# Threshold attention and a SoLU feed-forward block: extra matmuls into unread PSUM tiles before round 0 and in rounds 0 to 10

## The chip, the cores and the metric

The kernel runs on one core of a Trainium2 chip. The metric is device time in microseconds (us) of one execution; lower is better. A few per mille are enough to count here: three executions of the kernel before lie between 901.93 and 902.74 us.

## The reference

Attention over 8 batches of 8 heads, 576 positions of width 64, in float32, keeps only scores that lie within `tau` of their row's maximum. The result, seen as 4608 tokens of width 512, goes through a feed-forward block with a SoLU activation and a layer norm:

```python
scores = scale * np.matmul(q, k.transpose(0, 1, 3, 2))
thresh = np.max(scores, axis=-1, keepdims=True) - tau
scores = np.where(scores >= thresh, scores, -1000000000.0)
scores = scores - np.max(scores, axis=-1, keepdims=True)
attn = np.exp(scores)
attn = attn / (np.sum(attn, axis=-1, keepdims=True) + 1e-09)
x = np.matmul(attn, v)                  # then (B,H,S,D) -> (B*S, H*D)
h = x @ w_in                            # 512 -> 1024
solu = h * softmax(h)
ln = (solu - mu) / np.sqrt(var + 1e-06) * g_ln
out = ln @ w_out                        # 1024 -> 512
```

The weights `w_in` and `w_out` arrive as 64-bit floats; the kernel turns their bits into float32 on the chip.

## The kernel before

**Rounds.** The order of all work is written out by hand: one Python loop (L757 to L880) issues a round at a time, and every engine executes its own part of it in the order in which it was issued. There are 144 rounds with scores (`NS`), 18 for each batch; a round handles 128 query rows of two heads. After the last one the loop goes on until the feed-forward work is finished. In round `rnd` the loop issues, in this order:

1. `scores(rnd)` (L379): TensorE multiplies into the two PSUM tiles `s0` and `s1`, first the last 64 key columns, then the 512 others. All matmuls of the kernel but one work on 64 by 64 quarters of the array, four of them side by side (two halves of the rows, two of the columns); each float32 matmul appears in the profile as two rows.
2. `maxes(rnd)` (L411, its instruction is L417): VectorE finds each row's threshold. `ramp` (L428) on ScalarE applies it; `exps` (L437) on ScalarE takes the exponential and its sum.
3. In rounds 0, 2 and 4 only: `whole_pair(1)`, `whole_pair(2)`, `whole_pair(3)` (L358). TensorE transposes q, k and the row ends of two heads (L273) into two PSUM tiles, and ScalarE copies the results out to SBUF, six copies in the order q, q, k, k, ends, ends (L306, L331, L347, L351), alternately from the first tile and the second. `whole_pair(0)` stands before the loop and shares its copies between ScalarE and VectorE.
4. `normalise(rnd - 1)` (L441) on GpSimd.
5. One quarter of a feed-forward tile, if one is under way: `ff_h` or `ff_o`. The first becomes ready for round 11, so in rounds 0 to 10 the variable `quarter` stays 0, `cur` and `prev` stay None and so does `step`.
6. `attend` (L474), if a unit's weights are due (`LAG_PV`), in rounds 5, 7, 9, 10, 12 and on: TensorE multiplies the transposed weights `wT` with v (L495), and ScalarE copies the result out (L517).
7. `blocks(rnd - 1)` (L451): VectorE transposes the weights in blocks (L459), and DMAs put them in place in odd rounds.
8. In rounds 0 to 15: the conversion of one 128x512 piece of the weights, `weight_b` and then the first part of the next, `weight_a` (L217 to L253), mostly on VectorE, with one step on ScalarE (L230).

**PSUM.** Besides `s0` and `s1` there are two more tiles of 128x1024, named `p0` and `p1`, each with one buffer. The list `pairs_free` says which are to be had:

```python
    def take(name):
        tag = pairs_free.pop(0)
        return tag, ps_mm.tile([P, 1024], F32, tag=tag, name=name)
```

Who takes a tile puts its name back at the end of the list when the last reader has been issued; whether that reader has also finished is left to semaphores, which the framework sets: the first writer of a tile waits until the earlier tile of that name has been read. `whole_pair` takes both and gives both back, `attend` takes one and `attended` gives it back, and `gains()` (L186, round 3) takes and returns one.

**Before the loop.** The loads of the first two heads are issued, then `constants()` makes the identity matrix `ident` on GpSimd, further loads follow, and then `whole_pair(0)`.

Of the kernel before, what the change touches and what calls it, by code (L numbers as in the profile page):

```python
# [8 lines left out]
F32 = mybir.dt.float32  # L9
# [7 lines left out]
P = 128  # L17
# [3 lines left out]
def kernel(  # L21
# [27 lines left out]
    nc = tc.nc  # L49
# [50 lines left out]
    def take(name):  # L100
        tag = pairs_free.pop(0)
        return tag, ps_mm.tile([P, 1024], F32, tag=tag, name=name)


    def fence(first):
        m = nc.gpsimd.memset(mark, 0.0)
# [60 lines left out]
    def constants():  # L167

        nc.gpsimd.memset(lim, 0.0)
        nc.scalar.activation(out=ntau, in_=lim, func=AF.Exp)  # L170
        make_identity(nc, ident)
        nc.gpsimd.memset(mhalf, -0.5)
        nc.gpsimd.memset(mone, -1.0)
        nc.gpsimd.memset(lim, -896.0 * 8388608.0)

        nc.vector.tensor_scalar(
            out=scl, in0=tau_t, scalar1=0.0, scalar2=SCALE, op0=ALU.is_ge, op1=ALU.mult
        )  # L180
        nc.vector.tensor_scalar(
            out=tau_t, in0=tau_t, scalar1=0.0, scalar2=104.0, op0=ALU.max, op1=ALU.min
        )
        nc.vector.tensor_scalar(out=ntau, in0=tau_t, scalar1=-1.0, scalar2=None, op0=ALU.mult)
# [248 lines left out]
    def exps(s):  # L433
        d = live[s]
        d["sm"] = sm = small.tile([P, 2], F32, tag="sm", name="sm")
        for x, w in enumerate(d["w"]):
            nc.scalar.activation(  # L437
                out=w, in_=w, func=AF.Exp, bias=ntau, scale=1.0, accum_out=sm[:, x : x + 1]
            )
# [244 lines left out]
    NS = len(slots)  # L684
    PER = NS // B
    LAG_PV = 3

    pv_due = []
    for s, (b, kind, hp, r) in enumerate(slots):
# [39 lines left out]
    with tc.manual_schedule():  # L729
        nc.scalar.dma_start(out=tau_t, in_=tau.partition_broadcast(P))  # L730
        load_qk(0, 0)
        weight_load(0)
        constants()
        for x in range(1, 3):
            weight_load(x)
        for nm in ("q", "k"):
            load_ends(0, nm, slice(2, H), nc.sync)
        load_qk(0, 1)
        nc.sync.dma_start(out=g_rows, in_=g_ln.rearrange("(c p) -> c p", p=P))
        whole_pair(0)  # L740


        pieces = {r: x for x, r in enumerate(range(16))}
        whole = {0: 1, 2: 2, 4: 3}
        for r, hf, parts in ((0, 0, (0,)), (1, 0, (1, 2)), (3, 1, (0,)), (5, 1, (1, 2))):
            load_at[r] = [lambda hf=hf, parts=parts: load_v(0, hf, parts)]

        ready = []
        rnd = 0
        prev = cur = None  # L750

        between, starts, turns = [], [], []
        quarter = 0
        w2_done = False

        begin, middle, late = {}, {}, {}
        while True:  # L757
            more = rnd < NS
            if not more and not (
                ready or cur or prev or between or pv_due or live  # L760
                or max([rnd - 1, *begin, *middle, *late]) >= rnd
            ):
                break
            for job in begin.pop(rnd, []):
                job()
            if rnd == NS:
                pairs_free += ["s0", "s1"]
                if prev is not None:
                    between.append(prev)
                    prev = None  # L770
                if quarter == 2:
                    between.append(cur)
                    cur = None
                    quarter = 0
                assert quarter != 3
            if (
                cur is None and quarter == 0 and ready and ready[0][0] <= rnd
                and (more or len(between) < 3)
            ):
                cur = ready[0][1].pop(0)  # L780
                if not ready[0][1]:
                    ready.pop(0)
            busy = cur is not None or prev is not None
            items = []
            if more:
                room = SPARE
                if busy and quarter > 1 and preps and rnd + 4 < first_slot(preps[0][3]):
                    room = 0
                while preps and preps[0][0] <= rnd and preps[0][1] <= room:
                    _, n, make, _ = preps.pop(0)  # L790
                    items.append(make())
                    room -= n
                scores(rnd, items)
                maxes(rnd)
                ramp(rnd, 0)
                if rnd == 0:
                    weight_a(0)
                keeps(rnd, 0)
                keeps(rnd, 1)
                ramp(rnd, 1)  # L800
                exps(rnd)
            if rnd in whole:
                whole_pair(whole[rnd])
            if rnd - 1 in live:
                normalise(rnd - 1)
            for job in middle.pop(rnd, []):
                job()
            due = bool(pv_due) and pv_due[0][0] <= rnd
            step = None
            if quarter < 2 and cur is not None:  # L810
                step = ("h", quarter)
            elif quarter == 3:
                step = ("o", 1)
            elif not more:
                if between and ffn[between[0]].get("turned", NS + rnd) <= rnd:
                    prev = between.pop(0)
                    step = ("o", 0)
            elif quarter == 2 or (prev is not None and not due):
                if prev is None or (ffn[prev].get("turned", NS + rnd) <= rnd and w2_done):
                    step = ("o", 0)  # L820

            attending = None
            if due and (step is None or step[0] == "h") and len(pairs_free) > (step == ("h", 0)):
                attending = pv_due.pop(0)[1]
            if step == ("h", 0):
                ff_h(cur, 0, rnd + 1 < NS)
                quarter = 1
            elif step == ("h", 1):
                ff_h(cur, 1, None)
                quarter = 2  # L830
                late.setdefault(rnd, []).append(lambda t=cur: (ff_max(t), ff_exp(t)))
                late.setdefault(rnd + 1, []).append(lambda t=cur: (ff_mul(t), ff_sum(t)))
                middle.setdefault(rnd + 2, []).append(lambda t=cur: ff_stats(t))
                late.setdefault(rnd + 2, []).append(lambda t=cur: ff_norm(t))
                middle.setdefault(rnd + 3, []).append(lambda t=cur: (ff_norm2(t), ff_swap(t)))

                at = rnd + 4 if more or not ready else rnd + 6
                late.setdefault(at, []).append(lambda t=cur, at=at: ff_turn(t, at))
                if not more:
                    between.append(cur)  # L840
                    cur = None
                    quarter = 0
            elif step == ("o", 0):
                if prev is not None:
                    ff_o(prev, 0)
                quarter = 3
            elif step == ("o", 1):
                if prev is not None:
                    ff_o(prev, 1)
                    begin.setdefault(rnd + 1, []).append(lambda t=prev: ff_out(t))  # L850
                    late.setdefault(rnd + 1, []).append(lambda t=prev: ff_store(t))
                prev, cur = cur, None
                quarter = 0
            if attending is not None:
                attend(attending)
                attended(attending)
                b, kind, hp = attending
                if kind == 2 and b % 2:
                    ready.append((rnd + 1, [(b // 2,)]))
                elif kind < 2 and hp == NP - 1:  # L860
                    ready.append((rnd + 1, [(b, kind, 0), (b, kind, 1)]))
            if rnd - 1 in live:
                blocks(rnd - 1)
            for job in late.pop(rnd, []):
                job()
            if rnd == 3:
                gains()
            if rnd in pieces:
                x = pieces[rnd]
                weight_b(x)  # L870
                if x + 3 < len(pieces):
                    weight_load(x + 3)
                if x + 1 < len(pieces):
                    weight_a(x + 1)
            for job in load_at.pop(rnd, []):
                job()
            if rnd - 1 in pieces:
                weight_d(pieces[rnd - 1])
                w2_done = pieces[rnd - 1] == NW - 1
            rnd += 1  # L880
# [33 lines left out]
```

## Time and profile before

| what | value |
|---|---|
| median of three executions | 902.25 us (901.93 to 902.74) |
| the profiled execution, its own time | 902.25 us |
| its span, first to last instruction | 900.4 us |
| mean granted TensorE clock | 0.975 of full |
| TensorE matmul busy | 847.8 us (94%) |
| VectorE busy | 680.1 us (76%) |
| ScalarE busy | 591.9 us (66%) |
| GpSimd busy | 452.7 us (50%) |

PE is the matmul row of TensorE, PEld its weight loads, DVE is VectorE, ACT ScalarE, POOL GpSimd, SP the engine that issues most DMAs. Times in the timeline are in us from the start of the span: a row gives start, duration, engine, line, operation, the tiles written and read, shapes and count, and in brackets the idle time before it with what ended it. A start of round n is told here by the first of the two L417 rows of that round: 10.51 us for round 0, 15.27 for round 1, 21.25, 26.79, 32.13, 37.42, 43.86 for rounds 2 to 6, 104.59 for round 16.

### The profile page before, as it was taken

The page shows a single profiled execution, that of the slowest core. Times are in us where ns is not written, and L with a number is a line of the kernel's source. Part 1 is how long each engine was busy: PE and PEld are TensorE (multiplying, and loading weights), DVE is VectorE, ACT ScalarE, POOL GpSimd, SP SyncE. Part 2 cuts the span into 40 slices and gives each one's busy share as a digit, 9 for nine tenths or more (in the row PEclk, how much of TensorE's full clock was granted, in tenths as well). Part 3 has the DMA queues.
Part 4 walks back from the last instruction along what each step waited for, and adds up shares of the span by engine and source line. Part 5 has one row for each costly group of instructions (what it writes and reads, how often), then busy time and mean ns, then how long its engine had stood idle before and what let it go on. Part 6 is the DMA issues. An engine that isn't in the chain of part 4 may idle for free. (4 is left out here: it accounts for less than half of the span.)

```text
span 900.4 us, 39661 instructions
## 1 busy us (share of the span) xinstructions
PE 847.8 (94%) x17089; PEld 658.4 (73%) x17089; DVE 680.1 (76%) x1307; ACT 591.9 (66%) x1239; POOL 452.7 (50%) x870
## 2 busy tenths in 40 slices
PE   5667889999899999999999999999999999999997
PEld 3444677778688777877678787888778888777555
DVE  5999878878677777777777877777877877787351
ACT  5776767767677766777666766777767766666121
POOL 2556555555455555555545555555545555555120
PEclk8678899999999999999999999999999999999999
DMA  7999878886867777876767777876877766766322
GB/s 240 238 244 264 208 188 204 190 192 165 195 163 173 164 173 173 183 179 163 187 146 178 179 159 183 184 176 155 192 173 174 178 135 149 169 142 136 79 48 48
DMA packets 95502, 154.61 MB, mean 172 GB/s; under 512 B 27224, under 2 KB 69216, under 8 KB 95328
## 3 DMA queue, kind: packets, MB, share of 16 engines
q1 hardware_dynamic: 94336, 150.22, 70.5%
q8 instruction: 134, 2.20, 1.1%
q10 hardware_dynamic: 992, 1.87, 0.6%
q14 instruction: 40, 0.33, 0.1%
HBM read 46.14 MB, written 9.44 MB: 62 GB/s over the span
## 5 line engine op out<-in xcount | busy, mean ns | idle before, releaser
L417 DVE CUSTOM_DVE_ANT_0 w<-s_ps,tau_t 128x576 f32<-128x576 f32 x288 | 206.6, 755 | 151.3 <-PE s_ps L400 122.9
L428 ACT ACTIVATE w<-s_ps,nth 128x576 f32<-128x576 f32 x288 | 207.7, 744 | 121.4 <-DVE nth L417 100.1
L651 PE MATMUL o_ps<-w,uT 64*64 64x256 f32 x4608 | 271.3, 376 | 1.9 <-issue 1.0
L651 PEld LDWEIGHTS o_ps<-w,uT 64*64 64x64 f32 x4608 | 227.9, 133 | 51.2 <-ACT xh L517 9.6
L549 PE MATMUL h_ps<-w,xh 64*64 64x512 f32 x1856 | 222.0, 592 | 4.4 <-issue 4.4
L447 POOL TENSOR_SCALAR w<-w,sm 128x576 f32<-128x576 f32 x288 | 217.8, 768 | 14.3
L437 ACT ACTIVATE w<-w,ntau 128x576 f32<-128x576 f32 x288 | 220.3, 772 | 0.0
L459 DVE STREAM_TRANSPOSE T<-w 128x576 f32<-128x576 f32 x288 | 205.7, 750 | 4.3 <-POOL w L447 4.0
L495 PEld LDWEIGHTS pv<-wT,v 64*64 64x64 f32 x5760 | 173.5, 136 | 32.9 <-issue 13.8
L400 PE MATMUL s_ps<-kT,qT 64*64 64x64 f32 (+1 forms) x2048 | 177.1, 422 | 16.3 <-ACT w L428 15.1
L549 PEld LDWEIGHTS h_ps<-w,xh 64*64 64x64 f32 x1856 | 127.0, 134 | 80.8 <-issue 34.0
L495 PE MATMUL pv<-wT,v 64*64 64x128 f32 (+1 forms) x5760 | 173.9, 264 | 7.2 <-DMA wT<-T 5.1
L444 POOL TENSOR_SCALAR sm<-sm 128x2 f32<-128x2 f32 x144 | 36.1, 251 | 270.1 <-ACT w L437 267.4
L445 POOL TENSOR_TENSOR sm<-sm,mone 128x2 f32<-128x2 f32 x144 | 107.7, 748 | 12.0
L400 PEld LDWEIGHTS s_ps<-kT,qT 64*64 64x64 f32 x2048 | 70.2, 139 | 23.7 <-ACT w L428 21.0
L613 ACT ACTIVATE V<-u,nb,rs 128x1024 f32<-128x1024 f32 x36 | 44.7, 1241 | 52.4 <-POOL nb L603 52.4
L517 ACT COPY xh<-pv 128x256 f32<-128x256 f32 x64 | 23.8, 371 | 70.1 <-PE pv L495 70.1
L437 ACT ACTIVATION_READ_ACCUMULATOR w<-w,ntau 128x1 f32 x288 | 57.0, 198 | 0.0
L639 DVE STREAM_TRANSPOSE uT<-V 128x1024 f32<-128x1024 f32 x36 | 44.0, 1221 | 10.8 <-DMA V<-u 10.7
L562 DVE TENSOR_REDUCE hm<-h_ps 128x1 f32<-128x1024 f32 x36 | 43.0, 1195 | 10.7 <-PE h_ps L539 5.7
L577 DVE TENSOR_TENSOR u<-h_ps,u 128x1024 f32<-128x1024 f32 x36 | 42.8, 1190 | 10.6 <-ACT u L571 10.6
L571 ACT ACTIVATE u<-h_ps,hm 128x1024 f32<-128x1024 f32 x36 | 40.3, 1119 | 13.1 <-DVE hm L562 6.9
(74 smaller groups left out, 626.7 us busy)
## 6 DMA issues: line engine op xcount, KB each, us to landing
wT<-T SPq DMA_DIRECT2D x288, 288.0 KB, 5.6
V<-u SPq DMA_DIRECT2D x144, 64.0 KB, 3.6
out_dram<-ob SPq DMA_DIRECT2D x72, 128.0 KB, 3.1
v<-in_v_dram SPq DMA_DIRECT2D x16, 512.0 KB, 6.4
v<-in_v_dram SPq DMA_DIRECT2D x32, 256.0 KB, 5.9
q<-in_q_dram SPq DMA_DIRECT2D x15, 512.0 KB, 6.2
k<-in_k_dram SPq DMA_DIRECT2D x15, 512.0 KB, 6.8
raw<-in_moe_w_out_dram SPq DMA_DIRECT2D x8, 512.0 KB, 6.8
```

Of the source, the lines that this page charges most:

```text
L400: nc.tensor.matmul(out=ps[h][ROWS[y], ks], lhsT=lhsT, rhs=d["kT"][ROWS[h], ks], start=True, stop=True,)
L417: nc.vector.tensor_tensor_reduce(out=w, in0=ps[:, 0:S], in1=tau_t.to_broadcast([P, S]), scale=1.0, scalar=BIG, op0=ALU.add, op1=ALU.min, a ...
L428: nc.scalar.activation(out=d["w"][x], in_=d["ps"][x][:, 0:S], func=AF.Prelu, bias=d["nth"][x], scale=-1.0, alpha=1.0e30,)
L437: nc.scalar.activation(out=w, in_=w, func=AF.Exp, bias=ntau, scale=1.0, accum_out=sm[:, x : x + 1])
L445: nc.gpsimd.tensor_tensor(out=sm, in0=sm, in1=mone, op=ALU.pow)
L447: nc.gpsimd.tensor_scalar(out=w, in0=w, scalar1=sm[:, x : x + 1], scalar2=1.0, op0=ALU.mult, op1=ALU.mult)
L459: nc.vector.transpose(out=T[:, :, r, h, :], in_=w)
L495: nc.tensor.matmul(out=to, lhsT=d["v"][ROWS[u], h0 + h, m ^ 4 * u if m < 8 else m], rhs=rhs, start=m == 0, stop=m == NK - 1,)
L549: mm = nc.tensor.matmul(out=h[ROWS[y], f], lhsT=x[ROWS[r], c, ROWS[y]], rhs=w1_parts[ROWS[r], c, part ^ r], start=part == 0 and c == 0, st ...
L613: nc.scalar.activation(out=V, in_=u, func=AF.Identity, bias=nb, scale=rs)
L639: nc.vector.transpose(out=uT, in_=d["V"].rearrange("p y (m x) -> p m y x", x=32))
L651: nc.tensor.matmul(out=d["o"][ROWS[z], 512 * r : 512 * r + 256], lhsT=d["uT"][ROWS[r], m].rearrange("p y x -> p (y x)"), rhs=w2[ROWS[r], m ...
```

## The change

A helper `stir` issues four matmuls, one for each quarter of the array, into a fresh tile of a given PSUM name. No instruction reads that tile. It is called six times before `whole_pair(0)`, on `s0`, with the identity matrix as both operands and 128 columns; and in rounds 0 to 10 on the tile that stands first in `pairs_free` (the name is not taken from the list), with the identity and 512 columns of the first pair's `kT`. The first call in a round stands between `exps` and `whole_pair`, whenever `quarter` is 0 or 3; it is called A here. The second stands between the choice of `step` and `attend`, when the round has neither a feed-forward step nor a unit to attend; it is called B.

```diff
+    def stir(tag, cols, rhs_of):
+        x = ps_mm.tile([P, 1024], F32, tag=tag, name="stir")
+        for r in range(2):
+            for y in range(2):
+                nc.tensor.matmul(
+                    out=x[ROWS[y], 512 * r : 512 * r + cols], lhsT=ident[ROWS[r], ROWS[y]],
+                    rhs=rhs_of(ROWS[r]), start=True, stop=True,
+                )
...
     LAG_PV = 3
+    STIRRED = 10
...
         load_qk(0, 0)
         weight_load(0)
         constants()
+        for _ in range(6):
+            stir("s0", P, lambda rows: ident[rows])
         for x in range(1, 3):
             weight_load(x)
...
                 keeps(rnd, 1)
                 ramp(rnd, 1)
                 exps(rnd)
+            if more and rnd <= STIRRED and not quarter % 3:
+                stir(pairs_free[0], SM, lambda rows: pairs[0]["kT"][rows, 0:SM])
             if rnd in whole:
                 whole_pair(whole[rnd])
...
                 prev, cur = cur, None
                 quarter = 0
+            if rnd <= STIRRED and step is None and attending is None:
+                stir(pairs_free[0], SM, lambda rows: pairs[0]["kT"][rows, 0:SM])
             if attending is not None:
                 attend(attending)
                 attended(attending)
```

`SM` is 512 and `P` is 128. A is issued in rounds 0 to 10, B in rounds 0 to 4, 6 and 8.

## The prediction

> **What bounds the kernel now.** I read first the 40 slices of the page, because the change touches only rounds 0 to 10, the first 70 us.
>
> ```profile
> PE   5667889999899999999999999999999999999997
> ...
> DVE  5999878878677777777777877777877877787351
> ...
> PEclk8678899999999999999999999999999999999999
> ```
>
> TensorE has idle stretches only in the first six slices (135 us), and there its granted clock is low too. VectorE is the full engine there. The table of busy time by stage sharpens this (busy us of PE, PEld, DVE, ACT, POOL, then the clock):
>
> ```profile
> 20.00:25.00 5.00, 4.55 (x94) 2.88 (x86) 4.89 (x11) 3.84 (x10) 2.99 (x4) 0.67 0.66 201
> ...
> 100.00:110.00 10.00, 10.00 (x264) 7.68 (x260) 6.92 (x11) 5.83 (x17) 3.11 (x6) 1.00 0.70 169
> ```
>
> From 20 to 100 us VectorE is busy 4.87 to 5.00 of every 5 us, but for 40 to 45 (4.13). From 100 to 160 us TensorE is busy 8.5 to 10.0 of every 10, and the page has it at 9 from there to the end. So the front is set by VectorE's own work, the rest by TensorE's. VectorE executes in order: idle time put before one of its instructions in the front moves everything after it, TensorE's full stretch included. Idle time that is already there is all that a faster TensorE can win back.
>
> Third, the timeline of the front, for what TensorE waits for.
>
> ```profile
> 15.27 0.76 DVE L417 CUSTOM_DVE_ANT_0 w<-s_ps,tau_t 128x576 f32<-128x576 f32 x1
> ...
> 16.39 0.35 ACT L347 ACTIVATE qe<-tp,scl 128x64 f32<-128x64 f32 x1
> ...
> 26.18 0.34 ACT L347 ACTIVATE qe<-tp,scl 128x64 f32<-128x64 f32 x1
> ...
> 26.57 0.22 PE L188 MATMUL g_ps<-ident,g_rows 8*128 8x8 f32 x1 [1.80 <-ACT qe L347]
> 26.79 0.75 DVE L417 CUSTOM_DVE_ANT_0 w<-s_ps,tau_t 128x576 f32<-128x576 f32 x1
> ...
> 37.39 0.34 ACT L347 ACTIVATE qe<-tp,scl 128x64 f32<-128x64 f32 x1
> ...
> 37.79 4.22 PE L495 MATMUL pv<-wT,v 64*64 64x128 f32 x72 [1.80 <-ACT qe L347]
> ...
> 41.68 2.24 PE L400 MATMUL s_ps<-kT,qT 64*64 64x64 f32 x16
> ...
> 43.86 0.76 DVE L417 CUSTOM_DVE_ANT_0 w<-s_ps,tau_t 128x576 f32<-128x576 f32 x1 [0.83 <-PE s_ps L400]
> ```
>
> The two PE rows that end in "ACT qe L347" are the first users of a `p` tile after a `whole_pair`: each waited until ScalarE had made the copy of the ends, the last one out of that tile. Today both stand behind the next round's scores, and nothing urgent is queued behind them.
>
> **The change, part by part.** *Price of a stir.* The same shape runs in `ff_h`: weight loads of four rows follow each other every 0.85 us at half clock (95.34, 96.19, 97.04) and every 0.43 at full clock (98.59, 99.02, 99.45). A stir has eight rows: 1.70 or 0.86 us. From an unhindered start of the scores to VectorE's max it is 2.18 at half clock (41.68 to 43.86; 2.23 in round 0) and 1.24 or so at full (the row at 109.78, 1.24 long, ended when the max of 111.06 began).
>
> *B in rounds 0, 2 and 4.* `whole_pair` has just given its tiles back, so B writes the first of them, and like the two rows above it must wait for the copy of the ends. Queued behind it on TensorE are the next round's scores; behind those VectorE's max, then ScalarE's ramp, and so on. Before, the scores ran during ScalarE's copies. The new start of the max is: end of the copy, 0.05 us of signal, stir, scores.
>
> - Round 0: 16.39 + 0.35 + 0.05 = 16.79. With 0.86 + 1.24 the max starts at 18.89, with 1.70 + 2.23 at 20.72, against 15.27: 3.6 to 5.4 later. Round 1 holds 0.55 us of VectorE idle time (its row at 17.27 waited for GpSimd) that takes up as much: 3.1 to 4.9.
> - Round 2: copy's end 26.52, from the max at 21.25 5.27, a chain of ScalarE's own work that moves with the max. New period 5.32 + 2.10 = 7.42, or 5.32 + 3.93 = 9.25, against 26.79 - 21.25 = 5.54: 1.9 to 3.7.
> - Round 4: copy's end 37.73, 5.60 after the max at 32.13. New period 7.75 to 9.58 against 5.29: 2.5 to 4.3.
>
> Which clock? TensorE idles before B from the end of `whole_pair` (A moves it later) to the copy: some 3.4 us in round 0, 2.5 in round 2, 4 in round 4. Rows of before: after 3.16 idle (18.14), 1.64 (28.43, after one tiny matmul) and 3.4 (56.07) the scores ran at half clock; even after 1.80 idle the 72 rows at 37.79 took 4.22 us against 2.23 for 72 at 100.74. After 1.59 (45.51) they ran at full. Hence I take mostly half: 3.6 for stir and scores together in rounds 0 and 4, 3.2 in round 2. That gives 16.79 + 3.6 - 15.27 - 0.55 = 4.6, 5.32 + 3.2 - 5.54 = 3.0 and 5.65 + 3.6 - 5.29 = 4.0: **11.6 us**; the ends are 7.5 and 12.9.
>
> [...]
>
> *Round 5.* A, then `attend`, then the scores of round 6, on the path today: VectorE idles 0.83 us at 43.86 because those 72 rows ran at half clock. At full clock 0.86 + 2.23 + 1.24 = 4.3 fits into VectorE's own 5.6 us and the 0.83 goes; at half clock 1.70 + 4.22 + 2.23 = 8.15 against 6.44 costs 1.7. TensorE has by then worked some 4 us on end, so I take a gain of 0.4.
>
> *All other stirs of the loop (11 A and 7 B less the three)*: nothing. In rounds 1, 3, 6 and 8 A and B stand where TensorE waits for ScalarE's ramp: 2.3 us after the max the last ramp ends, the scores end 1.2 to 2.2 later, under the 5.3 of the period. In rounds 7 and 9 `attend` and the next scores end 1.77 and 1.82 us before VectorE needs them, against 0.86 to 1.70 for A; in round 10 `attend` waits for a DMA (0.86 and 1.66 us) behind A. At half clock throughout that cover is thin: two stirs (3.4) plus scores (2.2) exceed 5.3 by 0.3 us, a round at most 0.4; I keep 1.0 in all for the upper end.
>
> *The six before the loop.* The identity is complete at 1.32, the first q lands at 4.8. A matmul of 64 columns at half clock lasts 0.31 us, so one of 128 about 0.42 and a stir, two waves of four, about 0.65, as the tile is the same each time: 6 x 0.65 = 3.9, from 1.4 to 5.3. At worst `whole_pair(0)` starts 0.6 late. Against that the transposes (1.1 us for 32) and the scores of round 0 may find the full clock: 2.23 - 1.24 = 1.0 gained. I take 0.5 gained, between -1.0 and +0.6.
>
> *Later.* In rounds 16 and 17 VectorE idles 2.67 and 1.44 us for TensorE, whose clock was half from 85 to 98 us. No stir is issued there; but windows may fall otherwise after a shift. I take 0.5 gained, between -2.0 and 0.
>
> *Sum:* 11.6 - 0.4 - 0.5 - 0.5 = **10.2 us**. The profiled execution took 902.25 (span 900.4 and 1.85 around), which is also the median: **912.5**. Low ends: 7.5 - 0.8 - 1.0 - 2.0 = 3.7, 906; high ends: 12.9 + 1.7 + 0.6 + 1.0 = 16.2, 918.5.
>
> **The rivals.** *Warm and unhindered (faster):* B doesn't wait for the copies in effect, say because only unread columns matter, and the warm clock pays. It is bounded by VectorE's idle time: 1.0 in round 0, 0.83 at 43.86, up to 2.67 and 1.44 later: 896.3 to 900.4, say 899. It decides if B can start before about 12 us in round 0. Against it: B writes all 512 columns of both halves, the copies read columns 0 to 575, and the wait is seen twice. 0.06.
>
> *No change:* the delay is taken up before the end, because the full stretch of TensorE isn't tied to the front. For it speaks only that TensorE still idles 2.7 us between 120 and 140; every round follows the one before on each engine. 902. 0.04.
>
> *Slower, at full clock:* the stirs do keep the clock up, and stir and scores take 2.1 each time: 7.5 - 0.8 - 1.0 = 5.7, 908. 0.2.
>
> *Slower, the cover gone as well:* half clock throughout, rounds 1, 3 and 6 go over and `attend` in round 5 costs: 916 to 920. 0.12.
>
> **How the numbers follow.** The forecast has 0.58 and the range 906 to 918: it takes in the full-clock case and most of the last, leaving out the faster and unchanged cases and the very top. Something under 0.2% (1.8 us) a measurement of this kernel can't tell from no change; faster 0.06, same 0.04, slower 0.58 + 0.2 + 0.12 = 0.90.
>
> **What would show it.** In the timeline after: rows `stir` that waited for "ACT qe L347" after each of the three `whole_pair`s, with 2 to 4 us idle before them; the max of round 1 at 19 to 21 us instead of 15.27, that of round 6 near 54 instead of 43.86; VectorE idle "<-PE s_ps L400" of 2 to 5 us in rounds 1, 3 and 5; rounds 6 to 15 as long as before, and the whole stretch after 105 us the same, shifted. Matmul rows grow by 192 (24 stirs of eight). If the three waits are there and the end moves by less than 5 us, the step "a shift stays" is wrong; if the max of round 1 stays near 15, the step on the wait is.

## The result and the profile after

The changed kernel took 924.53 us (median of four executions, 921.16 to 927.05) against 902.5 us for the kernel before (901.93 to 904.42): a ratio of 1.0238 with a 95% interval of 1.0201 to 1.0275. The profiled execution took 927.05 us, its span 925.1, 24.7 more than before. It is slower, as forecast, but by 22 us instead of 10, above the top of the range (918). Timed again beside other kernels it came to 1.0194 (1.0141 to 1.0247). An execution more than 1.5% above the quickest of its kernel isn't counted in any ratio here, and the one profile of such an execution (64 pads in `whole_pair(1)`, 915.87 us) stands in no table.

The 40 slices of the page after the change; a slice is now 23.1 us:

```profile
PE   7588799989999999999899998999999999999997
...
DVE  3889987868777777787677776777877777777451
...
PEclk8899799999999999999999999999999999999999
```

TensorE's clock is up in the front (8899 in the first four slices, before 8678), VectorE is less busy there, and TensorE has three 8s in what was its full stretch. The 24.7 us have two parts. Comparing the start of each round's first L417 row (L426 in the changed file) with before: round 6 is 12.1 us late, and 12.1 it stays until round 15; round 16 is 11.0 late. From there to the end 13.8 us more are lost, for the most part in single jumps (2.2 at round 31, 3.5 at round 76, 5.2 at round 94), some of which are partly won back in the rounds behind them.

The front, in the timeline:

```profile
2.16 0.30 PEld L109 LDWEIGHTS stir<-ident 64*64 64x64 f32 x8 [0.49 <-PE stir L109]
...
17.65 1.98 PE L109 MATMUL stir<-kT,ident 64*64 64x512 f32 x8 [3.39 <-ACT qe L356]
...
21.59 0.76 DVE L426 CUSTOM_DVE_ANT_0 w<-s_ps,tau_t 128x576 f32<-128x576 f32 x1 [5.37 <-PE s_ps L409]
...
32.20 1.98 PE L109 MATMUL stir<-kT,ident 64*64 64x512 f32 x8 [4.69 <-ACT qe L356]
...
36.13 0.76 DVE L426 CUSTOM_DVE_ANT_0 w<-s_ps,tau_t 128x576 f32<-128x576 f32 x1 [3.89 <-PE s_ps L409]
...
47.14 1.98 PE L109 MATMUL stir<-kT,ident 64*64 64x512 f32 x8 [5.06 <-ACT qe L356]
...
50.71 0.76 DVE L426 CUSTOM_DVE_ANT_0 w<-s_ps,tau_t 128x576 f32<-128x576 f32 x1 [3.86 <-PE s_ps L409]
```

These are the three waits of B for ScalarE's copy of the ends, each followed by VectorE idle for the scores behind it. The first row is one of the six stirs ahead of the loop: each but the first waits 0.49 us for its forerunner, whose tile it reuses.

The late part, in the timeline (jumps at rounds 76 and 94), TensorE alone:

```profile
458.73 0.74 PE L504 MATMUL pv<-wT,v 64*64 64x64 f32 x35 [2.37 <-issue]
...
560.20 1.89 PE L660 MATMUL o_ps<-w,uT 64*64 64x256 f32 x27
565.35 3.85 PE L660 MATMUL o_ps<-w,uT 64*64 64x256 f32 x35 [3.27 <-issue]
```

Both times TensorE stops in the middle of a run of equal matmuls; no semaphore ended the stop ("issue"). And the busy time by stage, just after the first of them:

```profile
456.00:459.80 3.80, 1.43 (x74) 1.12 (x66) 0.00 (x0) 0.31 (x2) 2.40 (x4) 0.99 0.76 201
459.80:463.20 3.40, 3.40 (x20) 1.79 (x16) 2.18 (x6) 1.46 (x3) 0.00 (x0) 0.50 0.87 229
```

The granted clock (third from the end) is 0.50 for the next 3.4 us. Half the clock followed this stop; it didn't follow each: behind the longest of the kernel before, 2.17 us up to 447.1, the clock stood at 1.00 (447.0 to 450.6 us). TensorE's waits that end in "issue" between 110 and 850 us (us in total, times, longest), before:

```profile
PE h_ps L549 <- issue: 4.4, 3, 2.2
...
PE s_ps L273 <- issue: 1.5, 1, 1.5
...
PE o_ps L651 <- issue: 1.0, 2, 0.8
PE pv L495 <- issue: 0.2, 1, 0.2
```

and after:

```profile
PE pv L504 <- issue: 5.2, 3, 2.4
PE o_ps L660 <- issue: 5.0, 3, 3.3
...
PE s_ps L282 <- issue: 1.9, 2, 1.2
...
PE s_ps L409 <- issue: 0.3, 1, 0.3
```

With the shortest ones, from round 16 on, the profile before has 7.2 us of such stops and, up to the last scores, none of the half clock; the profile after has 13.4 us of stops (0.7 of them behind the last scores) and 10.2 us at half clock, in three stages of 3.4. In both traces the stretches between the first change of the clock and the last are whole multiples of 3.413 us; those at half clock last 3.4, 6.8, 10.2 or 13.7.

One of these three stages, at 196.9 us, stands behind no stop but behind a wait for a DMA:

```profile
196.04 0.44 PE L504 MATMUL pv<-wT,v 64*64 64x128 f32 x4 [1.62 <-DMA wT<-T]
197.22 3.58 PE L504 MATMUL pv<-wT,v 64*64 64x128 f32 x66 [0.74 <-DMA wT<-T]
```

That is the jump of 2.2 us at round 31. Nearly all kernels below have it there, the fastest of them (48 pads, no stirs) too:

```profile
186.67 3.33 PE L495 MATMUL pv<-wT,v 64*64 64x128 f32 x66 [0.44 <-DMA wT<-T]
```

In the profile before the same 66 rows took 2.07 us behind a wait of 1.06. So this jump doesn't follow the place of the code, which the next paragraph comes to.

**Where the stops fall.** The page lists packets of a queue that carries instructions:

```profile
q8 instruction: 136, 2.23, 1.1%
```

and before:

```profile
q8 instruction: 134, 2.20, 1.1%
```

Every one of these packets has 16,384 bytes, and TensorE's rows in the trace (weight loads, matmuls and waits for events), 34,827 now and 34,439 before, make 256 and 257 to a packet: 64 bytes a row. Counting those rows in order, I looked at which row each stop ends: 123 stops of over 50 ns in fifteen profiles of this study, and every one ends at a row whose number leaves 194 or 195 when divided by 256, 2.2 to 3.3 us after the latest packet of that queue began and 1.2 to 1.8 us after it ended. From these counts I take a packet for a piece of 256 of TensorE's instructions, and the stops for waits for the next piece; no row names what such a stop waits for. The change adds 388 instructions ahead of round 11 (96 matmuls of four rows each and 4 waits), one piece and 132; all code after them lies elsewhere against the pieces.

### The profile page after: what moved, and what is told of

The parts are those of the page before. It is cut to its first block, busy times and chain, and to the rows that moved or that the text cites. A ratio compares the mean times of both kernels' runs of the same rounds, so it can differ in the third digit from the quotient of the medians.

```text
span 925.1 us, 40049 instructions
## 1 busy us (share of the span) xinstructions
PE 868.4 (94%) x17281; PEld 646.5 (70%) x17281; DVE 679.5 (73%) x1307; ACT 591.6 (64%) x1239; POOL 451.9 (49%) x870
## 5 line engine op out<-in xcount | busy, mean ns | idle before, releaser
L426 DVE CUSTOM_DVE_ANT_0 w<-s_ps,tau_t 128x576 f32<-128x576 f32 x288 | 206.7, 755 | 179.6 <-PE s_ps L409 148.4
L660 PE MATMUL o_ps<-w,uT 64*64 64x256 f32 x4608 | 275.1, 378 | 6.7 <-issue 5.0
L660 PEld LDWEIGHTS o_ps<-w,uT 64*64 64x64 f32 x4608 | 223.9, 133 | 63.2 <-issue 14.2
L456 POOL TENSOR_SCALAR w<-w,sm 128x576 f32<-128x576 f32 x288 | 217.8, 768 | 14.3
L504 PEld LDWEIGHTS pv<-wT,v 64*64 64x64 f32 x5760 | 169.3, 134 | 39.0 <-issue 22.1
L504 PE MATMUL pv<-wT,v 64*64 64x128 f32 (+1 forms) x5760 | 171.5, 261 | 12.2 <-DMA wT<-T 6.0
L648 DVE STREAM_TRANSPOSE uT<-V 128x1024 f32<-128x1024 f32 x36 | 43.8, 1216 | 10.3 <-DMA V<-u 5.7
```

The lines of the kernel that those rows point to most:

```text
L426: nc.vector.tensor_tensor_reduce(out=w, in0=ps[:, 0:S], in1=tau_t.to_broadcast([P, S]), scale=1.0, scalar=BIG, op0=ALU.add, op1=ALU.min, a ...
L456: nc.gpsimd.tensor_scalar(out=w, in0=w, scalar1=sm[:, x : x + 1], scalar2=1.0, op0=ALU.mult, op1=ALU.mult)
L504: nc.tensor.matmul(out=to, lhsT=d["v"][ROWS[u], h0 + h, m ^ 4 * u if m < 8 else m], rhs=rhs, start=m == 0, stop=m == NK - 1,)
L648: nc.vector.transpose(out=uT, in_=d["V"].rearrange("p y (m x) -> p m y x", x=32))
L660: nc.tensor.matmul(out=d["o"][ROWS[z], 512 * r : 512 * r + 256], lhsT=d["uT"][ROWS[r], m].rearrange("p y x -> p (y x)"), rhs=w2[ROWS[r], m ...
```

## The experiments

Two theories for the front: the three waits, or the stirs' own work on TensorE. Two for the late part: the place of the code against the pieces, or a consequence of the late front. Ratios are against the kernel before, run beside each. "Late" means against the profile before. Pads are unread matmuls of 8 columns, four instructions each; their tile is written nowhere that is read.

### B in front of whole_pair

```diff
             if rnd in whole:
+                stir(pairs_free[0], SM, lambda rows: pairs[0]["kT"][rows, 0:SM])
                 whole_pair(whole[rnd])
...
-            if rnd <= STIRRED and step is None and attending is None:
+            if rnd <= STIRRED and rnd not in whole and step is None and attending is None:
```

> The changed kernel with the B of rounds 0, 2 and 4 issued in front of whole_pair instead of behind it; everything else, and the number of TensorE instructions (388 more than before), as in the changed kernel. Theory (wait): the three waits for ScalarE's copy of the ends made the 12.1 us by which round 6 starts later, so they go: round 6 starts within 1 us of 43.86. Theory (code): the further 12 us that the changed kernel loses after round 16 come from where the 16 KB pieces of TensorE's code begin (388 slots of 64 B is one piece of 256 and 132), so they stay: 910 to 915 us in all. Rival (work): the stirs' own TensorE time makes the front late, round 6 stays 6 us or more late, 917 to 925. Rival (late follows early): the later loss is a consequence of the front's delay, and goes with it: 900 to 904.

Measured: 1.0078 (1.0036 to 1.0120). VectorE's rows in its timeline, rounds 1 and 6:

```profile
16.61 0.76 DVE L426 CUSTOM_DVE_ANT_0 w<-s_ps,tau_t 128x576 f32<-128x576 f32 x1 [0.38 <-PE s_ps L409]
...
44.76 0.76 DVE L426 CUSTOM_DVE_ANT_0 w<-s_ps,tau_t 128x576 f32<-128x576 f32 x1 [0.82 <-PE s_ps L409]
```

Round 6 is 0.9 us late instead of 12.1, and those 0.9 are there from round 0 on (11.38 against 10.51): the same 24 stirs without the three waits cost the front only what the six ahead of the loop cost. The waits are shown. The wait for the copy itself is still there, at A of the next round, for which it is now the first writer:

```profile
17.65 0.66 PE L109 MATMUL stir<-kT,ident 64*64 64x512 f32 x4 [1.08 <-ACT qe L356]
```

but A stands behind the scores (from 15.41), and round 2 isn't later for it. What cost the 11 us was the place of the wait in TensorE's order. Most of the 7 us that remain are late ones.

### The changed kernel with 31 pads in whole_pair(1): 512 instructions

```diff
         for x, (_, make, _) in zip((0, 4, 8), items):
             make(spare, x)
+        if i == 1:
+            for j in range(31):
+                r, y = (j // 2) % 2, j % 2
+                nc.tensor.matmul(
+                    out=tiles[r][ROWS[y], 576 + 8 * (j // 4) : 584 + 8 * (j // 4)],
+                    lhsT=ident[ROWS[r], ROWS[y]], rhs=ident[ROWS[r], 64 * r : 64 * r + 8],
+                    start=True, stop=True)
```

> The changed kernel with 31 tiny unread matmuls of 8 columns (124 instruction slots) in whole_pair(1), ahead of its copies, where TensorE waits anyway: 512 slots more than before, exactly two pieces of code, so that all code after them lies against the pieces as it did before the change. Theory (code): the front's 12 us stay, the later loss goes: round 16 about 11 us late and the end 10 to 13 us late, 912 to 915 us; idle stretches of TensorE that no semaphore ended sum to about 7 us after round 16, as before. Rival (late follows early: a shift against DMA or the clock's windows): 920 to 927, as the changed kernel.

Measured: 1.0193 (1.0149 to 1.0237), no less than the changed kernel the second time. The theory's number was missed. Four of its eight stops from round 16 on stood where the four longest stand before the change, 512 rows farther (rows 4291, 8642, 17347 and 26050 for 3779, 8130, 16835 and 25538), but these four took 8.9 us in place of 5.9, and all eight 12.0.

### The kernel before with 33 and with 64 pads in whole_pair(1)

The same edit in the kernel before, which has no stirs: 132 and 256 instructions.

> The kernel before with 33 tiny unread matmuls (132 slots) in whole_pair(1), no stirs: the same place against the pieces of code as the changed kernel (388 - 256 = 132). Theory (code): the front moves by under 1 us, the later loss of some 11 us appears without any stir: 909 to 915 us. Rival: 902 to 903.

> The kernel before with 64 tiny unread matmuls (256 slots, exactly one piece of code) in whole_pair(1): control for the run with 33. Theory (code): 902 to 904 us, with TensorE's unexplained idle stretches at the same instructions as before. Rival (the extra matmuls themselves cost later): as far up as with 33 or farther.

Measured: 1.0084 (1.0057 to 1.0110) with 33 and 1.0066 (1.0025 to 1.0106) with 64: not told apart, though the run with 64 was the control and should have stayed at 902 to 904. The pads stood badly: in the profile with 33 TensorE already has a stop of 2.35 us in the middle of them, at 15.6 us, and round 1 is 2.8 us late. So the pair doesn't decide between the theories, and the pads were moved to round 8.

### The changed kernel again, and pads in round 8

```diff
+            if rnd == 8:
+                x = [ps_mm.tile([P, 1024], F32, tag=t, name="pad") for t in pairs_free]
+                for j in range(N):
+                    r, y = (j // 2) % 2, j % 2
+                    nc.tensor.matmul(
+                        out=x[r][ROWS[y], 8 * (j // 4) : 8 * (j // 4) + 8],
+                        lhsT=ident[ROWS[r], ROWS[y]], rhs=ident[ROWS[r], 64 * r : 64 * r + 8],
+                        start=True, stop=True)
             if attending is not None:
                 attend(attending)
```

> The changed kernel once more, unaltered, beside the others of this call: a measure for them, and for how much of its later loss comes back. The front should be late by the same 11 us at round 16. If the later loss is fixed by the program, 11 to 13 us again and 920 to 927 in all; if it is chance of the moment, anything from 913.

> The kernel before with 33 tiny unread matmuls in round 8, ahead of a stretch in which TensorE waits: 133 slots of code, no delay in the front (rounds 9 to 16 start within 0.3 us of before). Theory (code place): everything after lies against the 16 KB pieces as in the changed kernel, so 4 to 11 us slower than before. Rival (only delays and stalls in the front are paid for later): within 1 us of before.

> The same with 64 tiny matmuls, 257 slots, one piece of code and one slot. Theory (code place): within 2 us of before, clearly under the run with 33. Rival (only front delays): within 1 us of before and equal to the run with 33. Rival (any added instruction, wherever the pieces begin, costs later): 2 to 7 us slower, as the run with 33.

> All 24 stirs, B of rounds 0, 2 and 4 in front of whole_pair, and 31 tiny matmuls in round 8: 512 slots, two whole pieces. Theory (waits and code place together are the whole loss): about 1 us late in the front from the six stirs ahead of the loop, nothing after: 0 to 3 us slower than before. Rival (the late loss has another cause): 5 to 9 us slower, as when B was moved without the pad.

Measured: the changed kernel 1.0194 (1.0141 to 1.0247); before with 33 pads 1.0106 (1.0052 to 1.0161), with 64 pads 1.0027 (0.9976 to 1.0077); B in front of `whole_pair` and 31 pads 1.0035 (0.9980 to 1.0091). With 33 pads and no stir at all, and round 16 even 2.2 us early, 10.0 us are lost after round 16: the late loss needs no late front. With one whole piece more, and with two, the ratio isn't told from 1, but by the medians they are 4.2 and 4.5 us slower, more than the theory had allowed (within 2, and 0 to 3), and the profile with two loses 7.0 us after round 16, where nothing was expected. Nor do the intervals of these single comparisons part 33 from 64 by themselves.

### Other places, and the waits taken out

> The changed kernel with 31 tiny matmuls in round 8 (512 slots in all, two whole pieces of code): the run with the pad in whole_pair(1) once more, with the pad where it delays nothing. Theory (waits plus code place): the front 11 to 13 us late, little after it, 13 to 16 us slower than before (ratio 1.014 to 1.018). Rival (the later loss belongs to the delayed front): 18 to 22 us, as the changed kernel (1.020 to 1.024).

> The kernel before with 16 tiny matmuls in round 8: 65 slots, a quarter of a piece. If the loss depends on where the pieces begin, stretches of TensorE that no semaphore ended stand at other instructions than before and than with 133 slots, and the total may be anything from 4 us faster to 10 us slower. If any added instruction costs the same: equal to the runs with 133 and 257.

> The same with 48 tiny matmuls: 193 slots, three quarters of a piece. Expectations as for 65 slots: by the place of the pieces from 4 us faster to 10 us slower, and different from 65 and 133.

> All that costs taken out: B of rounds 0, 2 and 4 in front of whole_pair, no stirs ahead of the loop, 55 tiny matmuls in round 8 (513 slots, two pieces and one slot). Theory: round 0 starts at 10.5 us as before instead of 11.4, the front not late, the warm clock gains at most the 0.8 us of VectorE's idle time ahead of round 6; in all within 3 us of before, on either side. Rival (the warm clock does pay once nothing hinders it): 3 to 6 us faster than before.

The last one is B in front of `whole_pair` without the six stirs ahead of the loop:

```diff
-        for _ in range(6):
-            stir("s0", P, lambda rows: ident[rows])
```

Measured: the changed kernel with 31 pads in round 8 1.0129 (1.0096 to 1.0161), a little under what was expected: 11.8 us late at round 16, 1.4 more after it. Before with 16 pads 1.0075 (1.0044 to 1.0106); with 48 pads 0.9963 (0.9931 to 0.9995), **a little faster than both kernels**. The intervals at 16 and 48 are far apart, and so are those at 33 and 48; the edit is the same but for the number of dead matmuls. The waits of TensorE between 100 and 895 us in the profile with 48 pads, the largest that end in "issue" (us in total, times, longest):

```profile
PE s_ps L400 <- issue: 1.4, 1, 1.4
...
PE h_ps L549 <- issue: 0.7, 1, 0.7
PE s_ps L273 <- issue: 0.2, 1, 0.2
```

and in the profile with 16 pads (here between 100 and 910 us):

```profile
PE s_ps L273 <- issue: 5.0, 2, 2.8
PE pv L495 <- issue: 4.5, 3, 2.5
...
PE s_ps L400 <- issue: 1.3, 2, 0.7
```

The version with every known cost of the front taken out came to 1.0009 (0.9984 to 1.0034). Round 0 starts at 10.71, and at 10.3 to 10.9 in every other profile without the six stirs; with them it is 11.4 each time. So they cost most of the 0.87 us. Round 6 starts 0.7 early, the idle time of 0.83 ahead of it gone, and that was lost again by round 9. The clock itself did become warm: this version from 13 to 67 us, and below it the kernel before (busy us of PE, PEld, DVE, ACT, POOL, then the clock):

```profile
13.00:67.00 54.00, 42.63 (x843) 20.90 (x835) 52.15 (x110) 41.95 (x93) 29.89 (x40) 1.00 0.93 240
...
13.00:67.00 54.00, 34.42 (x549) 23.45 (x553) 52.07 (x110) 42.03 (x93) 29.58 (x40) 0.72 0.90 239
```

VectorE was busy for 52 of these 54 us without it already. And even the 0.7 us can't be credited to the stirs. The kernels with 33 and with 16 pads in round 8 do, up to there, what the kernel before does, without a stir; their profiles have lost the idle time ahead of round 6 as well. With 33 pads, TensorE's scores, 1.20 us for 16 rows where the kernel before took 2.24, and VectorE's row behind them:

```profile
41.01 1.20 PE L400 MATMUL s_ps<-kT,qT 64*64 64x64 f32 x16
...
42.77 0.75 DVE L417 CUSTOM_DVE_ANT_0 w<-s_ps,tau_t 128x576 f32<-128x576 f32 x1
```

In reverse, B in front of `whole_pair` has all 24 stirs and kept 0.82 us of it.

### Three quarters of a piece, with the stirs

> The changed kernel with 15 tiny matmuls in round 8: 448 slots, one piece and three quarters, the place at which the kernel before was at its best (193 slots). Theory (code place): the front 12 to 13 us late, then 3 to 4 us won back against before: 7 to 10 us slower than before in all (ratio 1.008 to 1.011), unexplained idle of TensorE after round 16 some 2 to 4 us. Rival (the delayed front is paid for later): 1.013 or more.

> All 18 stirs of the loop with B of rounds 0, 2 and 4 in front of whole_pair, none ahead of the loop, 39 tiny matmuls in round 8: 449 slots. Theory (code place): 2 to 5 us faster than the same at 513 slots, ratio 0.995 to 0.999 against before. If the warm clock is worth anything in the front, under the 0.996 of the kernel before with 193 slots; if not, equal to it. Rival (place doesn't matter): 1.001 as at 513 slots.

Measured: the changed kernel with 15 pads (448 instructions) 1.0113 (1.0083 to 1.0142): 11.8 us late at round 16, as every version with the three waits, and 1.2 won back after it. That is a little above what was expected; its interval just touches that of the changed kernel's second timing (from 1.0141). The version without waits at 449 instructions came to 1.0002 (0.9979 to 1.0025), not the 0.995 to 0.999 expected: its late part did gain 1.1 us, but round 16 was 4.6 us late in its profile, by a jump of 3.2 at round 11 and smaller ones, which I didn't follow.

The profiles by place (instructions added, their remainder by 256; loss after round 16 against before; stops from round 16 on; half clock from round 16 to the last scores):

| remainder | kernel | added | after round 16, us | stops, us | half clock, us |
|---|---|---|---|---|---|
| 0 | before | 0 | 0 | 7.2 | 0 |
| 1 | 64 pads, round 8 | 257 | +4.7 | 7.2 | 10.2 |
| 0 | changed, 31 pads in whole_pair | 512 | +8.8 | 12.0 | 6.8 |
| 0 | changed, 31 pads in round 8 | 512 | +1.4 | 5.9 | 6.8 |
| 0 | B in front, 31 pads | 512 | +7.0 | 10.1 | 10.2 |
| 1 | B in front, no six, 55 pads | 513 | +4.9 | 8.6 | 6.8 |
| 65 | 16 pads, round 8 | 65 | +13.4 | 11.8 | 10.2 |
| 132 | changed | 388 | +13.8 | 13.4 | 10.2 |
| 132 | changed, again | 388 | +10.6 | 11.5 | 6.8 |
| 132 | B in front | 388 | +14.3 | 14.0 | 10.2 |
| 132 | 33 pads in whole_pair | 132 | +3.3 | 5.4 | 3.4 |
| 133 | 33 pads, round 8 | 133 | +10.0 | 11.7 | 3.4 |
| 193 | 48 pads, round 8 | 193 | -3.0 | 2.4 | 3.4 |
| 192 | changed, 15 pads | 448 | -1.2 | 3.5 | 3.4 |
| 193 | B in front, no six, 39 pads | 449 | -1.1 | 4.1 | 3.4 |

With and without stirs, with and without a late front, the place near 192 wins 1 to 3 us and the place of the changed kernel loses 3 to 14. Each row is one execution set against one of the kernel before, whose own times span 898.7 to 912.5 us in this study; the intervals above say how much of it is more than chance. The stops beyond the 7.2 us of before plus half of the time at half clock come within 1.0 us of the loss at the remainders 0, 1, 192 and 193; at 65, 132 and 133 they leave 2.4 to 3.8 us of it open. What sets the size within one remainder (1.4 to 8.8 us at whole pieces) stays open. In the stage from 562.0 to 565.4 us of the changed kernel, which holds its longest stop, the DMA engines' share was 1.02; whether other transfers held up the packet there isn't shown.

## Why the prediction was right or wrong

**B's waits: right.** Period of each round, before and after, against the step as taken:

| step | forecast | measured |
|---|---|---|
| round 0 to 1 (without round 0's own delay) | +5.1 | 4.76 to 10.22: +5.5 |
| idle time of round 1 taken up | -0.55 | 5.98 to 5.29: -0.7 |
| round 2 to 3 | +3.0 | 5.53 to 9.25: +3.7 |
| round 4 to 5 | +4.0 | 5.28 to 9.22: +3.9 |
| round 5 to 6 | -0.4 | 6.44 to 5.28: -1.2 |
| six stirs ahead of the loop | -0.5 | +0.9 |
| round 16 | -0.5 | 8.15 to 7.01: -1.1 |
| sum at round 16 | 10.2 | 11.0 |

From the start of B to the max it took 3.9 us in rounds 0 and 2 and 3.6 in round 4, against 3.6, 3.2 and 3.6 as forecast: half clock for stir and scores in rounds 0 and 2 (granted 0.50 in both stretches, 0.58 in round 4's). In round 2 TensorE's wait was 4.69 us, where I had worked out 2.5. In round 5 the 71 rows of `attend` took 2.26 us, full clock (1.00 from 51.0 to 55.0 us). That some 4 us of work on end bring it was my estimate and isn't shown: before, TensorE was busy from 37.79 to 43.8 us on end, and the clock was 0.50 throughout. The rows of rounds 5 to 6 and 16 are right in sign, but not shown to be gains of the stirs: without any, 33 pads in round 8 have -0.9 and -1.1 there.

**The six stirs: wrong in sign.** I sized a stir at 0.65 us and let the clock repay it. They follow each other every 0.79 us, for each waits for its forerunner to finish; `whole_pair(0)` started at 5.8 instead of 4.9, and its transposes took 1.08 us for 32 against 1.13: a row still took 0.31 us, as long as before, where such rows take 0.22 us at full clock (L273 at 102.9 us, before).

**The other stirs of the loop: right.** Rounds 6 to 14 keep their lengths to 0.06 us, behind the covers named.

**After round 16: the step that failed** is "the whole stretch after 105 us the same, shifted". It holds for the order of the work, not for TensorE's code. The 192 more matmul rows were in the prediction as a number to check and had no price. What was lost there is 13.8 us in the profiled execution, most of what the forecast lacked; by the medians of the two timings (22.0 and 18.9 us, less 11.0 and 11.6 at round 16) it is some 11 and 7. Of the 13.8, 6.2 us are more stops, and the half clock is worth some 5.1 by an estimate (half of 10.2), a third of it behind the wait for a DMA; 2.5 us stay open. That the place of the code behind an added block matters is shown by the pads: 16 dead matmuls cost some 7 us, 48 gain 3, and 31 or 15 in the changed kernel itself bring it from 1.019 and more to 1.013 and 1.011. That the place alone fixes the size is not shown: 31 pads in `whole_pair(1)` gained nothing. The profile before had the sign of it: its groups list TensorE idle time "<-issue" (4.4 us before `h_ps` alone), which I had passed over.

**The rivals.** "Warm and unhindered" fell with the three rows of B in the timeline, and the run without waits shows what it was worth: at most 0.7 us in the front, which runs without stirs reach too. "No change" fell as well. "Cover gone" had the size nearest the result, 916 to 920, but for a reason that didn't occur.

## What to carry to other kernels

Behind `whole_pair` the unread writes still waited for their PSUM tile, 3.39, 4.69 and 5.06 us, and held up the scores queued behind them on TensorE: 11 us for three waits. Issued ahead of the tile's next user, the same writes cost the front nothing. So ask of an unread write, too, when its tile comes free. A warmer TensorE had only the idle time to win here that the bounding engine already spent waiting for it, under 2 of 54 us: read that sum first, and before crediting a gain look for it in a run without the change. In this long program, written out without loops, an edit ahead moved the code behind it against the packets of 256 instructions, and profiles that differ in this ranged from -3 to +14 us: test an edit to such a program at several pad lengths before crediting or blaming it.

## What the hardware showed that I had not expected

- The instruction queue `q8` moved 136 packets of 16,384 bytes, one for every 256 of TensorE's 34,827 rows; all 123 stops of over 50 ns without a semaphore end at a row that leaves 194 or 195 when divided by 256, and the longest lasts 3.43 us. A stop of 2.37 us was followed by 3.4 us at half the clock, one of 2.17 us wasn't.
- The kernel before repeated within 0.3% in its first four executions, but spread from 898.7 to 908.9 us in 16 others and from 900.1 to 912.5 in 26 more. So a few per mille, which the first three executions seemed to resolve, are told only with many executions beside each other.
- Of the six stirs on one tile ahead of the loop, each from the second on stood 0.49 us until the matmuls of the one before had ended.
